# Tail scores ahead of the logits' weights in an attention and mixture-of-experts kernel, and the reads of their bank behind both

## The chip, the cores and the metric

The kernel runs on one core of one Trainium2 chip. The metric is the device time of one execution in microseconds (us), less is better. Every timed execution also records the span of its trace and the mean granted clock of TensorE. The quoted time is the median of a kernel's executions, "faster" and "slower" begin at 2%.

## The reference, cut to what matters

Causal attention over 8 batches x 8 heads, 576 positions of 64 elements, with a bias per pair of positions; then a mixture of 8 experts, in which each token goes to one expert.

```python
scores = scale * np.matmul(q, k.transpose(0, 1, 3, 2))
scores = np.where(causal, -1000000000.0, scores + np.minimum(bias, 0.0))
attn = np.exp(scores - max); attn = attn / (sum(attn) + 1e-09)
x = np.matmul(attn, v)                       # then (B, S, H*D)
logits = x @ w_gate; local_gate = sigmoid(x @ w_local)
# e = argmax(logits), or the expert of the token before where local_gate >= 0.5
out[b, s] = p[e] * (np.maximum(x[b, s] @ w1[e], 0.0) @ w2[e])
```

(shortened; `p` is the softmax of the logits.)

## The kernel before: the parts that matter

Attention goes over 32 pairs of heads, n = 0 to 31. 576 positions are four blocks of 128 and a tail of 64. The scores of the tail against itself are made apart, into columns of bank 1 of PSUM. The same bank takes the product of v with the weights of the logits ("gate"), and the tail's half of the product of the weights with v. The tokens' expert logits therefore come out of attention as extra columns of v.

In what follows, for pair n, S is its scores (L328), R the products of its weights with v (L402), G its products of v with the logits' weights (L366) and T its tail's scores (L351). A pass is the time from S of pair n to S of pair n + 1. PSUM, in banks, is where the program has TensorE put its products. In lines of the profile PE is TensorE, DVE VectorE, ACT ScalarE, POOL GpSimd and SP SyncE; "<-" in brackets names what ended a wait, and "issue" says that the profile shows nothing that was waited for. Each of these products stands in a trace as two records (the 20 of G as x40).

```python
def tail(n):
    ps = banks[1][:, TAIL : TAIL + TL]
    for h in range(2):
        d = slice(DH * h, DH * h + DH)
        mm(ps[d], lhsT=ins[n][1][:, TS:][:, d], rhs=ins[n][0][:, TS:], start=True, stop=True)   # L351
    sc = scs[n, "tail"] = p_sc.tile([P, TL], F32, name="tail")
    i = tail_bias + n
    nc.scalar.activation(sc, ps, Act.Exp, bias=bias[:, i : i + 1], scale=scale)                 # L354

def seen_tail(n):                                                                               # L358, on DVE
    ...
def gate_part(n):
    ps = banks[1][:, GATE : ...]
    ...                                     # 20 small products, bank 1 (L366)
    v = ins[n][3]
    nc.vector.tensor_copy(v[:, :, 1 : E + 2], ps[:, :, 0])                                      # L369
    nc.vector.tensor_copy(v[:, :, VW - E - 2 : VW - 1], ps[:, :, 1])                            # L370

def rows(n, g):                             # bank g
    ...                                     # products with v (L402), reciprocal (L404), multiply (L407)
    if g == 0 and hp == HP - 1:
        logits(b)                           # four DVE instructions, once in four pairs

tail(0)
for n in range(NPAIR + 1):
    load(n + 3)
    if n:
        seen_tail(n - 1)
    if n < NPAIR:
        for u, pieces in enumerate(...):    # three units
            scores(n, u)                    # L328
            weights(n, *pieces)             # 14 activations (L337) in all
    for f in plan.pop((n, 0), ()):
        f(bank)
    if n:
        rows(n - 1, 1)
        rows(n - 1, 0)
    ...
    if n < NPAIR:
        gate_part(n)
    if n + 1 < NPAIR:
        tail(n + 1)
    for half in (1, 2):
        for f in plan.pop((n, half), ()):
            f(bank)
```

(cut.) The `plan` holds the sort of the tokens: for four groups of batches, (0, 1), (2, 3), (4) and (5), their tokens' rows are scattered by expert while attention goes on, with indirect transfers that GpSimd issues, three in a pair of heads from n + 3 2/3 on (`i += 11`, L1018). The batches that are left follow after attention. Then come the experts.

## Time and profile before

| quantity | value |
|---|---|
| timed executions | 917.92, 919.64, 915.09 us |
| the execution that the profile shows | 860.34 us, span 858.6 us |
| TensorE busy | 813.0 us, 95% |
| TensorE waiting for L370, in T | 31.2 us, 31 times |
| attention ends | 295.35 us |
| sort's end and experts, after it | 563.2 us |

The profiled execution is not one of the timed ones and was 55 to 59 us faster than those.

### The profile page before, as it was taken

How to read it: one execution, taken by the hardware profiler on the slowest of the kernel's cores; microseconds unless marked ns; L12 is line 12 of the kernel's file. 1: busy time of each engine (PE TensorE's matmuls, PEld its weight loads, DVE VectorE, ACT ScalarE, POOL GpSimd, SP SyncE). 2: the span in 40 equal slices, each digit the busy share in tenths (PEclk: the TensorE clock that was granted, in tenths of full speed). 3: DMA queues.
4: the chain of work that ended last, by engine and by line, in shares of the span. 5: the costliest groups of instructions: out<-in, count | busy, mean ns of one | idle time of the engine just before them, and what ended most of it. 6: DMA issues, size and time to landing. Idle time of an engine off the chain costs nothing.

```text
span 858.6 us, 21153 instructions
## 1 busy us (share of the span) xinstructions
PE 813.0 (95%) x8793; PEld 603.9 (70%) x8793; DVE 210.3 (24%) x700; ACT 192.1 (22%) x535; POOL 174.1 (20%) x329
## 2 busy tenths in 40 slices
PE   9988989889888999999999999999999999999996
PEld 8777778777777885685667756676657756776762
DVE  2222432344343465301111111111111111111111
ACT  5655646557555300000000000000000000000000
POOL 3422235225434223101100011100011001100001
PEclk9999999999999999999999999999999999999999
DMA  9475448857555439996599566993689936996001
GB/s 317 141 234 159 156 138 269 319 197 226 188 165 215 168 107 333 402 396 216 179 359 391 217 235 227 360 386 146 236 302 379 371 132 231 322 409 235 20 14 40
DMA packets 64153, 204.64 MB, mean 238 GB/s; under 512 B 8269, under 2 KB 8301, under 8 KB 64048
## 3 DMA queue, kind: packets, MB, share of 16 engines
q1 hardware_dynamic: 55008, 172.41, 57.3%
q0 software_dynamic: 8896, 30.47, 9.4%
q8 instruction: 71, 1.16, 0.6%
q10 hardware_dynamic: 144, 0.33, 0.1%
q14 instruction: 34, 0.28, 0.1%
HBM read 179.93 MB, written 23.76 MB: 237 GB/s over the span
## 4 chain that ended last, share of the span: by engine, by line
PE 92%; DVE 3%; issue 2%; DMA 1%; ACT 1%; SPq 0%; POOL 0%; another core or an unknown queue 0%; POOLq 0%; ACTq 0%
PE yp L1200 31%; PE hp L1176 28%; PE o L402 12%; PE ps L328 11%; PE hp L1183 4%; PE xp L1059 2%; PE o L351 1%; PE o L366 1%; PE o L284 1%; DMA v<-in_vx_dram 1%; DVE v L369 1%; PE bank L930 1%; DMA x_rows<-r_empty 1%; PE bank L952 1%; DVE x L407 0%
## 5 line engine op out<-in xcount | busy, mean ns | idle before, releaser
L1200 PE MATMUL yp<-w,hT 128*128 128x512 f32 (+1 forms) x528 | 221.1, 594 | 0.0
L1176 PE MATMUL hp<-xT,w 128*128 128x256 f32 (+1 forms) x1088 | 192.1, 337 | 0.0
L1176 PEld LDWEIGHTS hp<-xT,w 128*128 128x128 f32 x1088 | 172.2, 191 | 23.7 <-issue 7.8
L337 ACT ACTIVATE sc<-ps,bias 128x256 f32<-128x256 f32 (+3 forms) x448 | 153.0, 471 | 36.4 <-PE ps L328 35.5
L1200 PEld LDWEIGHTS yp<-w,hT 128*128 128x128 f32 (+1 forms) x528 | 88.1, 181 | 100.4 <-issue 99.4
L1191 ACT ACTIVATE hT<-hp 128x512 f32<-128x512 f32 x38 | 22.7, 597 | 503.2 <-PE hp L1176 419.3
L1207 POOL DMA_INDIRECT out_dram<-y,at_gate x38 | 38.4, 1011 | 457.9 <-DVE y L1206 443.1
L402 PE MATMUL o<-v,sc 128*64 128x74 f32 x3072 | 113.9, 229 | 0.1
L402 PEld LDWEIGHTS o<-v,sc 128*64 128x64 f32 x3072 | 108.9, 136 | 7.3 <-issue 7.1
L328 PE MATMUL ps<-q,k 64*128 64x320 f32 (+2 forms) x768 | 102.5, 418 | 0.0
L343 POOL TENSOR_SCALAR_AFFINE_SELECT sc<-sc 128x256 f32<-128x256 f32 x160 | 65.8, 416 | 140.1 <-ACT sc L337 90.3
L328 PEld LDWEIGHTS ps<-q,k 64*128 64x128 f32 x768 | 77.2, 208 | 18.2 <-issue 2.7
L1189 DVE TENSOR_SCALAR hT<-hp 128x512 f32<-128x512 f32 x38 | 26.2, 689 | 220.4 <-PE hp L1176 187.7
L1200 PE MATMUL yp<-x,hT 128*128 128x512 f32 (+1 forms) x144 | 64.8, 595 | 0.0
L1206 DVE TENSOR_SCALAR y<-yp,at_gate 128x512 f32<-128x512 f32 x38 | 28.5, 751 | 135.5 <-PE yp L1200 135.5
L404 DVE RECIPROCAL recs<-o 128x4 f32<-128x4 f32 x64 | 12.1, 189 | 157.2 <-PE o L402 157.2
L1176 PEld LDWEIGHTS hp<-xT,x 128*128 128x128 f32 x320 | 46.1, 191 | 5.8 <-issue 2.6
L1176 PE MATMUL hp<-xT,x 128*128 128x128 f32 (+1 forms) x320 | 50.1, 317 | 0.0
L1018 POOL DMA_INDIRECT x_rows<-x,r_slot_i x40 | 38.7, 967 | 35.7 <-PE ps L328 19.7
L1067 DVE COPY xT<-xp 128x512 f32<-128x512 f32 x36 | 24.9, 691 | 81.1 <-PE xp L1059 81.0
L351 PE MATMUL o<-q,k 128*64 128x64 f32 x128 | 10.9, 250 | 31.2 <-DVE v L370 31.2
L1200 PEld LDWEIGHTS yp<-x,hT 128*128 128x128 f32 (+1 forms) x144 | 24.7, 178 | 21.3 <-issue 21.0
(160 smaller groups left out, 428.8 us busy)
## 6 DMA issues: line engine op xcount, KB each, us to landing
w<-in_w_dram SPq DMA_DIRECT2D x184, 512.0 KB, 9.7
x<-in_w_dram SPq DMA_DIRECT2D x56, 512.0 KB, 9.8
v<-in_vx_dram SPq DMA_DIRECT2D x32, 370.0 KB, 4.8
vt<-in_vz_dram SPq DMA_DIRECT2D x32, 320.0 KB, 3.5
k<-in_kz_dram SPq DMA_DIRECT2D x31, 320.0 KB, 5.1
q<-in_q_dram SPq DMA_DIRECT2D x32, 288.0 KB, 6.6
xg<-x_rows POOLq DMA_DIRECT2D x30, 293.0 KB, 8.5
x_rows<-r_empty SPq DMA_DIRECT2D x6, 293.0 KB, 5.4
```

The costliest lines, as they stand in the source:

```text
L328: mm(ps[:, h, at : at + z - a], lhsT=kb[d, c * P : c * P + P], rhs=qb[d, a:z], start=True, stop=True)
L337: nc.scalar.activation(scs[n, u][:, h, at : at + z - a], raw[u][:, h, at : at + z - a], Act.Exp, bias=bias[:, i : i + 1], scale=scale)
L343: nc.gpsimd.affine_select(out=x, in_=x, compare_op=Alu.is_ge, fill=0.0, base=0, pattern=[[0, 2], [1, P]], channel_multiplier=-1)
L402: mm(y, lhsT=w, rhs=x, start=start, stop=stop)
L1018: self.s.nc.gpsimd.indirect_dma_start(out=next(self.s.views)[:, :], out_offset=bass.IndirectOffsetOnAxis(ap=self.slot[:z, m : m + 1], axis=0),
L1067: nc.vector.tensor_copy(self.xT[i][:, :, k * P : k * P + P], self.ps)
L1176: mm(y, lhsT=w[0][:, c, f : f + P], rhs=xT[i][:, c, :], start=(c == 0), stop=(c == DK - 1))
L1183: mm(y[d, m], lhsT=w[h ^ swap][:, c, f + h * HALF : f + h * HALF + HALF], rhs=xT[i][:, c, m], start=(c == 0), stop=(c == DK - 1))
L1189: nc.vector.tensor_scalar_max(to, ps, 0.0)
L1200: mm(ps[n * m : n * m + m, :], lhsT=hT[i][:, c, a : a + m], rhs=wn[:, c, :], start=(c == 0), stop=(c == FK - 1))
L1206: nc.vector.tensor_scalar_mul(y, ps, gate[i, k])
L1207: nc.gpsimd.indirect_dma_start(out=next(outs)[:, :], out_offset=bass.IndirectOffsetOnAxis(ap=at[i, k][:, 0:1], axis=0), in_=y[:, :], eleme ...
```

## The change

The intent: T no longer waits for DVE to copy G's result out of their common bank, since T now comes before G; both copies come after both products. The logits no longer stand ahead of the copies on DVE. ACT's read of the tail goes behind the activations of the first unit of the next pass. The five scatters of the last group (batch 5) come one pair later.

```diff
-                i += 11
+                i += 11 if bs[-1] < 5 else 14
...
-    tail(0)
+    tail_scores(0)
     for n in range(NPAIR + 1):
         load(n + 3)
-        if n:
-            seen_tail(n - 1)
         if n < NPAIR:
             for u, pieces in enumerate((((0, 0), (3, 1)), ((0, 1), (1, 1)), ((2, 0), (2, 1), (1, 0)))):
                 scores(n, u)
                 weights(n, *pieces)
+                if u == 0:
+                    tail(n)
+            seen_tail(n)
...
+        if n + 1 < NPAIR:
+            tail_scores(n + 1)
         if n < NPAIR:
-            gate_part(n)
-        if n + 1 < NPAIR:
-            tail(n + 1)
+            gate_parts(n)
+            beside_v(n)
+        if n and n % HP == 0:
+            logits(n // HP - 1)
```

(cut: `tail` was split into `tail_scores`, the products, and `tail`, the activation; `gate_part` into `gate_parts`, the products, and `beside_v`, the copies; the call of `logits` left `rows`.)

More of the change, by code (lines that the diff above doesn't have):

```diff
@@ L344, in weights, with tail_scores, tail @@
                                             pattern=[[0, 2], [1, P]], channel_multiplier=-1)
-    def tail(n):
-        ps = banks[1][:, TAIL : TAIL + TL]
+    def tail_scores(n):
         for h in range(2):
             d = slice(DH * h, DH * h + DH)
-            mm(ps[d], lhsT=ins[n][1][:, TS:][:, d], rhs=ins[n][0][:, TS:], start=True, stop=True)
+            mm(banks[1][d, TAIL : TAIL + TL], lhsT=ins[n][1][:, TS:][:, d], rhs=ins[n][0][:, TS:], start=True, stop=True)
+    def tail(n):
         sc = scs[n, "tail"] = p_sc.tile([P, TL], F32, name="tail")
         i = tail_bias + n
-        nc.scalar.activation(sc, ps, Act.Exp, bias=bias[:, i : i + 1], scale=scale)
+        nc.scalar.activation(sc, banks[1][:, TAIL : TAIL + TL], Act.Exp, bias=bias[:, i : i + 1], scale=scale)
     def seen_tail(n):
@@ L358, in seen_tail, with gate_parts @@
         nc.vector.scalar_tensor_tensor(x, x, 3e38, seen, Alu.min, Alu.mult)
-    def gate_part(n):
-        ps = banks[1][:, GATE : GATE + NB * 2 * (E + 1)].rearrange("p (c h e) -> p c h e", c=NB, h=2)
+    gates = banks[1][:, GATE : GATE + NB * 2 * (E + 1)].rearrange("p (c h e) -> p c h e", c=NB, h=2)
+    def gate_parts(n):
         m = P // 4
@@ L365, in gate_part, with beside_v @@
             for j in range(0, P, m):
-                mm(ps[j : j + m, c], lhsT=ins[n][2][:, c * P + j : c * P + j + m], rhs=wz[:, n % HP],
+                mm(gates[j : j + m, c], lhsT=ins[n][2][:, c * P + j : c * P + j + m], rhs=wz[:, n % HP],
                    start=True, stop=True)
+    def beside_v(n):
         v = ins[n][3]
-        nc.vector.tensor_copy(v[:, :, 1 : E + 2], ps[:, :, 0])
-        nc.vector.tensor_copy(v[:, :, VW - E - 2 : VW - 1], ps[:, :, 1])
+        nc.vector.tensor_copy(v[:, :, 1 : E + 2], gates[:, :, 0])
+        nc.vector.tensor_copy(v[:, :, VW - E - 2 : VW - 1], gates[:, :, 1])
     def rows(n, g):
@@ L407, in rows @@
         nc.vector.tensor_tensor(x, y, rec.unsqueeze(3).to_broadcast([P, t1 - t0, 2, HW]), op=Alu.mult)
-        if g == 0 and hp == HP - 1:
-            logits(b)
     def logits(b):
```

## The prediction

> **What bounds the kernel now.** I read the page first (parts 1, 4 and the tail rows of part 5), then what TensorE waits for, then the timeline of one ordinary pair of heads, then the chain in order of time, then the clock by stretches. Names used below: for pair n, S(n) is its scores (L328), R(n) its products with v (L402), G(n) its products of v with the logits' weights (L366), T(n) its tail scores (L351). TensorE runs, per pass, S(n), R(n-1), G(n), T(n+1).
>
> ```profile
> span 858.6 us, 21153 instructions
> PE 813.0 (95%) x8793; PEld 603.9 (70%) x8793; DVE 210.3 (24%) x700; ACT 192.1 (22%) x535; POOL 174.1 (20%) x329
> ...
> PE 92%; DVE 3%; issue 2%; DMA 1%; ACT 1%; SPq 0%; POOL 0%; another core or an unknown queue 0%; POOLq 0%; ACTq 0%
> ...
> L351 PE MATMUL o<-q,k 128*64 128x64 f32 x128 | 10.9, 250 | 31.2 <-DVE v L370 31.2
> ```
>
> TensorE is the bound, 95% busy, 92% of the chain, so only time at which it stands still or runs slowly can be won. The last row is nearly all its recorded idle time: T waits 31.2 us in all for the second DVE copy (L370) that takes G's result out of PSUM. The list of TensorE's own waits says how often, and that nothing else comes near:
>
> ```profile
> PE o L351 <- DVE v L370: 31.2, 31, 2.2
> PE hp L1183 <- issue: 4.3, 3, 1.8
> PE o L284 <- POOL ident masks.py:199: 1.5, 1, 1.5
> ```
>
> One ordinary pass, lines from the timeline (start, us, engine, line; in brackets the idle time before):
>
> ```profile
> 21.50 0.54 PE L366 MATMUL o<-wz,vt 128*32 128x18 f32 x40
> 21.61 0.20 DVE L404 RECIPROCAL recs<-o 128x6 f32<-128x6 f32 x1 [0.48 <-PE o L402]
> 21.84 0.61 DVE L407 TENSOR_TENSOR x<-o,recs 128x438 f32<-128x438 f32 x1
> ...
> 22.48 0.19 DVE L370 COPY v<-o 128x45 f32<-128x45 f32 x1
> ...
> 22.73 0.34 PE L351 MATMUL o<-q,k 128*64 128x64 f32 x4 [0.69 <-DVE v L370]
> 23.00 2.86 PE L328 MATMUL ps<-q,k 64*128 64x320 f32 x24
> 23.11 0.31 ACT L354 ACTIVATE tail<-o,bias 128x64 f32<-128x64 f32 x1 [1.91 <-PE o L351]
> 24.24 4.78 ACT L337 ACTIVATE sc<-ps,bias 128x320 f32<-128x320 f32 x14 [0.81 <-PE ps L328]
> ```
>
> G is done at 22.04, but DVE must finish the reciprocal and the multiply of R first, so its copies end at 22.67 and T starts 0.06 us later: 0.69 us of TensorE idle. In passes with scatters it is about 0.95 us, and once in four passes, where the four DVE instructions of the logits stand ahead of the copies, about 2 us.
>
> There is a second, less visible loss. In the chain most S blocks take 2.79 us, but seven take 4.18, 4.38, 4.41, 4.44, 4.45, 4.32 and 4.21, at 48, 82, 109, 153, 181, 218 and 266 us. The view by stretches (us, busy time of PE, PEld, DVE, ACT, POOL, then the granted clock) explains it:
>
> ```profile
> 44.02:47.43 3.41, 1.31 (x65) 1.13 (x59) 2.55 (x10) 0.53 (x2) 0.79 (x2) 1.00 1.02 166
> 47.43:50.84 3.41, 3.27 (x18) 2.60 (x20) 0.21 (x2) 0.99 (x3) 0.00 (x0) 0.50 1.01 392
> 105.46:108.87 3.41, 2.72 (x81) 2.41 (x77) 1.35 (x5) 1.03 (x4) 1.03 (x4) 1.00 0.46 150
> 108.87:112.28 3.41, 3.41 (x20) 2.75 (x21) 1.30 (x7) 1.12 (x3) 0.43 (x3) 0.50 0.34 125
> 115.70:119.11 3.41, 1.70 (x76) 1.51 (x71) 2.62 (x10) 0.34 (x2) 0.60 (x2) 1.00 0.43 128
> 119.11:122.52 3.41, 3.19 (x28) 2.70 (x30) 2.11 (x11) 1.40 (x4) 0.00 (x0) 1.00 0.53 178
> ```
>
> Stretches of 3.41 us follow each other on a fixed grid; after a poor one the next runs at half clock. Five of the seven poor ones hold the long wait of a logits pass or one like it (1.3 to 1.7 us busy); the other kind (105.46) holds a 0.69 us wait plus G and a run of tiny sort products (L952, 1.3 us)[...]. A stretch with 1.70 us busy (115.70) escaped[...].
>
> [...] T writes other columns than L369 and L370 read, and yet waits, 31 times. So every read of this bank, ACT's of the tail included, orders TensorE's later writes. [...] here gaps of about 2 us within a window were enough (longest wait 2.2)[...].
>
> **The change, part by part.**
> 1. T(n+1) moves ahead of G(n), the copies behind both. T then needs of DVE only that R(n-1)'s part in this bank (done first in R) has been multiplied out. That is old: G stood there before and had the same need, and shows no DVE wait in the list. Removed: the 31 waits, -31.2 us.
> 2. The long gaps go, and the hold passes lose their 0.69 us, so I expect the poor stretches to go[...]. Seven S blocks sum to 30.39 us against 7 x 2.79 = 19.53: -10.9 us.
> 3. T streams behind R, which has the same 128x64 array tiling, and not after a standstill. From T's start to S's took 0.27 (22.73 to 23.00); in R an instruction costs 3.49 / 96 = 0.036, so four cost 0.15. About 0.1 x 31 = -3 us (estimate).
> 4. ACT's read of the tail moves from before the 14 activations to after the first four. Here lies the new wait: R(n-1) begins with the tail's bank, so it must wait for that read. In the pass above S starts at 23.00, R at 25.79. ACT begins at 24.24; the four take until 25.68 or so (the fifth one's start), the tail's activation 0.31, until 25.99, and the signal 0.06: R can start at 26.05, 0.26 us late. Nothing stands beside it on TensorE. 31 x 0.26 = +8.1 us.
> 5. In passes where the sort puts ACT work ahead (L941: ACT begins 1.60 us after S and not 1.24; L908 waits on DVE, which is now relatively later), the same wait grows by some 0.3 to 0.4, in about eight passes: +3 us (estimate).
> 6. The copies and the logits come later on DVE, but v is needed by R(n) only one S (2.79 us) later, and DVE is 34% busy in this stage: 0. The tail's masking (L358) gets earlier: the one 0.8 us wait of R on it goes; counted as nothing.
> 7. The last early group's five scatters move a pair later. Now the first one holds POOL 6.5 us for the early fetch of rows, and the masks of a pair queue behind it; that costs TensorE nothing today, with the passes 8 to 9 us long, but would be close with 7.3. A safeguard: 0.
>
> Sum: -31.2 - 10.9 - 3 + 8.1 + 3 = -34 us, all in the first 295 us. The expert stage (563 us, clock 1.00) has the same instructions and begins that much earlier. The timed 917.9 is 59 us above the profiled span; I take this as fixed. 917.9 - 34 = 883.9; I add 1 for one half-clock window that survives: 885 us.
>
> **The rivals.** (a) The wait moves wholly to ACT: if the tail's read is later than I place it, by 0.5 us or more, R stands 0.7 us or more in each pass and the change gives back over 20 us: about 898. Against it: ACT needs 14 activations plus a tail, 4.78 + 0.31 = 5.1 us, in a pass of about 7.3, so it does not fall behind. (b) The half-clock windows stay[...]: about 896. For it: the hold passes triggered with only 0.69 us of true idle. Against: the logits passes lose 2 us of true idle. (c) POOL or the loads become the bound. POOL in a scatter pass: five masks of 0.41 and three scatters of about 1.3 with their gaps, about 6 us, under 7.3. The loads of a pair are 1.3 MB, 178 GB/s at 7.3 us, where the trace moves 400 elsewhere, and they are issued three pairs ahead. If wrong: about 900. (d) No new wait at all, if the guard were by columns: about 875; the 31 waits of today speak against it.
>
> **Range and chances.** Items 1 and 2 are measured, and each can fail only in part; the sizes of 4 and 5 are the loose ones, perhaps 6 us either way, and the windows up to 8 the wrong way. Range 879 to 894. The 2% line lies at 899.6, 19 us of gain: it takes (a) or (c) to miss it. Faster 0.94, within 2% 0.055, slower 0.005.
>
> **What would show it.** The row of T without idle; a new row of waits of L402 on ACT's tail activation, about 31 times and 0.3 us; S blocks all near 2.8 us and the clock 1.00 from 15 us to the end of attention; ordinary passes 7.3 us apart instead of 7.76; the experts' 563 us unchanged; no scatter waiting for the early fetch. Wrong if R waits 0.6 us or more, if T waits for R's multiply (L407), if several stretches at 0.50 remain, or if the span fell by over 40 us.

## The result, and the profile after

| | before | changed |
|---|---|---|
| timed, median | 916.5 us (4 runs, 914.04 to 919.64) | 863.56 us (4 runs, 858.44 to 870.36) |
| ratio | | 0.9425, 95% interval 0.9346 to 0.9504 |

A ratio is the mean time of one kernel's runs over that of the other's of the same rounds, so not quite the ratio of the medians. The kernel became faster by 53 us. The predicted time was 885 us, with a range of 879 to 894; the result lies 15 us below the range.

Three lines of the changed kernel's page answer to those shown of before (busy times; the chain's shares; the group R, which has the line L406 now):

```profile
PE 811.8 (95%) x8793; PEld 600.0 (70%) x8793; DVE 214.5 (25%) x700; ACT 188.3 (22%) x535; POOL 173.4 (20%) x329
...
PE 89%; ACT 6%; issue 3%; DVE 1%; POOL 0%; POOLq 0%; ACTq 0%; DVEq 0%
...
L406 PE MATMUL o<-v,sc 128*64 128x74 f32 x3072 | 115.5, 231 | 17.1 <-ACT tail L355 15.7
```

T no longer stands idle, ACT stands in the chain with 6%, and R waits for ACT's tail activation: the old wait is gone and the expected new one is there, with 15.7 us instead of the 11 predicted. But the span of this profile is 856.8 us and that of the profile before was 858.6: the two profiles differ by 1.8 us, the two medians by 53. Two readings were open. Either the change gains little in the span and much outside it, or the two profiles are of different conditions. The second predicts that, on one and the same chip, spans and times of both kernels differ by the same amount.

### The profile page after: what moved, and what is told of

Its sections match the earlier page's. It is cut to its first block, busy times and chain, and to the rows that moved or that the text cites.

```text
span 856.8 us, 21067 instructions
## 1 busy us (share of the span) xinstructions
PE 811.8 (95%) x8793; PEld 600.0 (70%) x8793; DVE 214.5 (25%) x700; ACT 188.3 (22%) x535; POOL 173.4 (20%) x329
## 4 chain that ended last, share of the span: by engine, by line
PE 89%; ACT 6%; issue 3%; DVE 1%; POOL 0%; POOLq 0%; ACTq 0%; DVEq 0%
PE yp L1207 31%; PE hp L1183 28%; PE o L406 13%; PE ps L328 7%; ACT sc L337 5%; PE hp L1190 4%; PE xp L1066 2%; PE o L368 2%; PE o L284 1%; PE bank L959 1%; PE bank L937 1%; ACT tail L355 1%; PE o L349 1%; DVE r_u L947 0%; ACT r_v L948 0%
## 5 line engine op out<-in xcount | busy, mean ns | idle before, releaser
L337 ACT ACTIVATE sc<-ps,bias 128x256 f32<-128x256 f32 (+3 forms) x448 | 156.9, 482 | 80.4 <-PE ps L328 78.3
L406 PE MATMUL o<-v,sc 128*64 128x74 f32 x3072 | 115.5, 231 | 17.1 <-ACT tail L355 15.7
L406 PEld LDWEIGHTS o<-v,sc 128*64 128x64 f32 x3072 | 110.7, 138 | 26.4 <-ACT tail L355 24.4
L328 PEld LDWEIGHTS ps<-q,k 64*128 64x128 f32 x768 | 72.8, 189 | 26.5 <-issue 11.3
L1190 PEld LDWEIGHTS hp<-xT,w 128*64 128x64 f32 x768 | 30.9, 138 | 6.2 <-issue 6.2
L411 DVE TENSOR_TENSOR x<-o,recs 128x292 f32<-128x292 f32 x64 | 34.5, 538 | 2.2
```

The source lines that it names most:

```text
L328: mm(ps[:, h, at : at + z - a], lhsT=kb[d, c * P : c * P + P], rhs=qb[d, a:z], start=True, stop=True)
L337: nc.scalar.activation(scs[n, u][:, h, at : at + z - a], raw[u][:, h, at : at + z - a], Act.Exp, bias=bias[:, i : i + 1], scale=scale)
L406: mm(y, lhsT=w, rhs=x, start=start, stop=stop)
L411: nc.vector.tensor_tensor(x, y, rec.unsqueeze(3).to_broadcast([P, t1 - t0, 2, HW]), op=Alu.mult)
L1190: mm(y[d, m], lhsT=w[h ^ swap][:, c, f + h * HALF : f + h * HALF + HALF], rhs=xT[i][:, c, m], start=(c == 0), stop=(c == DK - 1))
```

## The experiments

Thirteen runs. Kernels of one call ran on one chip and share the runs of the kernel before.

| run | chip | before, us | this, us | ratio | 95% interval |
|---|---|---|---|---|---|
| e1 before again | 4 | 863.17 | 862.24 | 1.0004 | 0.9948 to 1.006 |
| e2 changed again | 4 | 863.17 | 827.38 | 0.9584 | 0.9539 to 0.9629 |
| e3 scatters alone | 4 | 863.17 | 864.34 | 1.001 | 0.9956 to 1.0063 |
| e4 order alone | 4 | 863.17 | 829.51 | 0.9624 | 0.9581 to 0.9667 |
| e5 early read | 1 | 862.48 | 823.18 | 0.9547 | 0.9509 to 0.9585 |
| e6 changed, third | 1 | 862.48 | 828.73 | 0.9593 | 0.9544 to 0.9641 |
| e7 filled waits | 1 | 862.48 | 852.09 | 0.9878 | 0.9838 to 0.9918 |
| e8 logits later | 1 | 862.48 | 847.62 | 0.9825 | 0.9784 to 0.9866 |
| e9 before, other chip | 15 | 912.55 | 911.15 | 0.9985 | 0.9822 to 1.0147 |
| e10 changed, other chip | 15 | 912.55 | 856.76 | 0.9389 | 0.9217 to 0.956 |
| e11 before, scatters moved | 3 | 912.1 | 912.67 | 1.0012 | 0.9966 to 1.0058 |
| e12 changed, scatters moved | 3 | 912.1 | 863.59 | 0.9474 | 0.9418 to 0.953 |
| e13 early read again | 3 | 912.1 | 836.37 | 0.9175 | 0.908 to 0.9271 |

Theory A: the predicted mechanism is complete (about 34 us), and the first measurement met a condition in which the kernel before loses more. Rival B: part of the change that was taken for nothing (the scatters, the place of the logits) is worth 20 us. Rival C: the timed executions carry a cost outside the span that the change removes. (In the expectations of e1 and e2, "theory A" is another one: the fixed cost outside the span, as the prediction had it.)

### Both kernels again, and the two parts of the change (e1 to e4)

e1 and e2 are the two kernels without an edit. e3 is the kernel before with the scatters' line alone, e4 the changed kernel without it:

```diff
# e3, from before                              # e4, from changed
-                i += 11                       -  i += 11 if bs[-1] < 5 else 14
+                i += 11 if bs[-1] < 5 else 14 +  i += 11
```

> The unchanged kernel once more. Question: is its profiled span of 858.6 us (execution 860.3) typical, with 916 us in the timed executions? Theory A (a fixed cost outside the trace, as I had predicted): the profiled execution again near 860 and the timed ones near 916 with spans near 859. Theory B (the kernel before has a slower mode that its first profile missed): timed spans near 915 with a lower granted clock or more standing still inside the span, and with luck this profile falls into it. Ratio to the kernel before 1.00 either way.

> The changed kernel once more. Theory A: profiled and timed executions between 858 and 870 again, clock 0.98 to 0.99. Stalls of 1 to 5 us that the first profile shows at TensorE without a releaser (for instance at 132 and 190 us) are either at the same instructions again (then they belong to the program[...]) or elsewhere (then they belong to the execution).

> The kernel before with the last early group's five scatters one pair later and nothing else. My theory: this part alone is a safeguard and gives nothing (within 0.5% of before, 910 to 920 timed). Rival: the scatter that holds POOL 6.5 us, waiting for the early fetch of rows, is what puts the kernel before into its slow timed mode; then this one is near 865.

> The changed kernel with the scatters left where they were. My theory: all of the gain is in the order of the tail scores, so within 0.7% of the changed kernel (858 to 872). Rival: as above, then near 900 or more.

On this chip the kernel before took 863.17 us, not 917, and the changed kernel 827.38: 35.8 us less. The timed figures that the expectations of e1 to e4 had for these kernels (about 916, 858 to 870, 910 to 920, 858 to 872) were all missed, since they were those of the first measurement. (e3's 864 is near what its rival named, but the kernel before took as long on this chip.) The profiled and the timed executions of e1 agree (863.13 and a median of 862.24), which neither of its theories had. Spans moved with it, from 861.4 to 826.4 (-35.0). Rival C falls: what the timed runs show, the span shows. The prediction's own sum, taken from its own profile, 858.6 - 34 = 825, meets the span of 826.4. Rival B falls for the scatters: alone they moved nothing (ratio 1.001), and with the new order they gave 2.1 us at most (829.51 against 827.38), with intervals that overlap; whether that is real stays open. Both runs are of an ordinary chip. What the later scatters are worth in the slower condition was not run.

One ordinary pass of the changed kernel, from e2's timeline (start, us, engine, line; idle time before in brackets), answers the pass in the prediction:

```profile
58.52 0.54 PE L368 MATMUL o<-wz,vt 128*32 128x18 f32 x40
...
58.99 2.86 PE L328 MATMUL ps<-q,k 64*128 64x320 f32 x24
...
60.23 1.57 ACT L337 ACTIVATE sc<-ps,bias 128x320 f32<-128x320 f32 x4 [2.32 <-PE ps L328]
...
61.68 0.33 ACT L355 ACTIVATE tail<-o,bias 128x64 f32<-128x64 f32 x1
...
62.06 0.99 PE L406 MATMUL o<-v,sc 128*64 128x74 f32 x24 [0.21 <-ACT tail L355]
```

S follows G at once: 58.99, within the recorded span of G, where before T stood still for 0.69 us. ACT starts S's first four activations 1.24 us after S, reads the tail at 61.68 to 62.01, and R starts 0.05 us later. S would have let R start at 61.78 (2.79 us after 58.99, as before), so R is late by 0.28 us; the bracket calls 0.21 of it idle, since the recorded end of S is a little later. From S to S this pass lasts 66.13 - 58.99 = 7.14 us, before 7.76.

The rows that carry the sum, first of e1, then of e2 (busy us, mean ns; idle us before, and what ended it):

```profile
L328 PE MATMUL ps<-q,k 64*128 64x320 f32 (+2 forms) x768 | 102.8, 419 | 0.0
...
L351 PE MATMUL o<-q,k 128*64 128x64 f32 x128 | 10.8, 248 | 30.0 <-DVE v L370 30.0
```

```profile
L406 PE MATMUL o<-v,sc 128*64 128x74 f32 x3072 | 113.6, 229 | 7.5 <-ACT tail L355 6.9
...
L328 PE MATMUL ps<-q,k 64*128 64x320 f32 (+2 forms) x768 | 95.2, 392 | 2.8 <-issue 2.4
```

Read together: T's 30.0 us gone, R's 6.9 us new, S shorter by 7.6 us because the blocks at half clock went (seven stretches at half clock in attention before, one after; the mean granted clock of that stage went from 0.96 to 0.99). The question that e2 put, whether TensorE's waits without a releaser ("issue") come again at the same instructions, has an answer: those of 0.3 us and more in attention stand in passes 15, 18, 29 and 31 both in e2 and in e6 on another chip (e2 has one more in pass 23, e6 one in pass 20), the one in pass 18 in the middle of G (1.01 and 1.55 us). Most of them thus belong to the program; what they wait for is not shown.

### Two losses and the new wait, one at a time (e5 to e8)

e7 leaves T's waits in place and fills the long ones with products of the identity that nobody reads, so that only the clock can gain:

```diff
# e7, from before
         if n < NPAIR:
             gate_part(n)
+        if n in (4, 8, 11, 16, 19, 20, 12, 23, 24, 27, 28):
+            idle = bank(1)[0]
+            for i in range(6 if n % HP == 0 else 2):
+                mm(idle[:, :P], lhsT=ident, rhs=ident, start=True, stop=True)
```

e8 takes from the change only the place of the logits on DVE; e5 lets ACT read the tail right behind DVE's copies, before the next S has activations; e6 is the changed kernel unedited, beside them.

```diff
# e8, from before: the call of logits leaves rows, and
         if n < NPAIR:
             gate_part(n)
+        if n and n % HP == 0:
+            logits(n // HP - 1)
# e5, from changed
     tail_scores(0)
+    tail(0)
...
-                if u == 0:
-                    tail(n)
...
             beside_v(n)
+        if n + 1 < NPAIR:
+            tail(n + 1)
```

> The changed kernel, but ACT's read of the tail stands right behind DVE's copies, ahead of the pair's 14 activations, where ACT is idle. My theory: the new wait of R on the tail's activation (0.27 us in each of 31 passes) goes, nothing takes its place, so about 7 to 8 us less than the changed kernel, ratio to before near 0.950 where the changed kernel is at 0.958. Rival: the read now waits for the copies of DVE in the same bank and pushes the 14 activations back, so that nothing is gained or the scores' buffers come free too late (ratio 0.96 or more).

> The changed kernel a third time, beside the others, and on whichever chip this call gets. If the chip is like the one of the second run: 827 us and ratio 0.958. If it is like the one of the first (before at 916): 864 and 0.943, and then its profile shows more standing still of TensorE without a releaser, most of it in the first 290 us.

> The kernel before with its waits left as they are, but the long ones (logits passes) and those of the sort's hold passes filled with 6 and 2 products that nobody reads, so that TensorE is busy while it waits. My theory: the half-clock windows go, the waits stay (31 of them, about 30 us less what the fill covers), and the kernel gains 8 to 11 us, ratio 0.987 to 0.991. Rival: half clock costs nothing of its own because the slow scores are hidden behind ACT; then ratio 1.00.

> The kernel before with nothing changed but the place of the logits' four DVE instructions: behind the copies and not ahead of them. My theory: the seven long waits fall from about 2.0 to 0.7 us (about 9 us) and the four or five half-clock windows behind them go (about 7 us): 14 to 17 us, ratio 0.980 to 0.984; 31 waits remain, of about 0.7 to 0.95 us. Rival: the windows stay, since G and the wait still make a poor stretch: ratio 0.989 or more.

e7 gained 10.4 us (862.48 to 852.09) by adding work; by the 2% rule it counts as the same and e8 as unclear, but the intervals of both exclude a ratio of 1. Its row of S says why:

```profile
L328 PE MATMUL ps<-q,k 64*128 64x320 f32 (+2 forms) x768 | 93.7, 389 | 0.3 <-issue 0.3
```

S fell from 102.8 to 93.7 us, and one stretch of attention instead of seven ran at half clock (mean granted clock of the stage 0.99, in e1 0.96). That is close to the predicted -10.9, alone and on purpose.

e8 gained 14.9 us: T's waits fell from 30.0 to 24.4 us, S from 102.8 to 94.8.

```profile
L351 PE MATMUL o<-q,k 128*64 128x64 f32 x128 | 10.7, 246 | 24.4 <-DVE v L370 24.4
```

The place of the logits, of which the prediction spoke only as the long wait once in four passes, is therefore a large part: it shortens six of the seven long waits to 0.7 us (that of pass 4 stays at 2.2) and leaves two stretches at half clock in attention instead of seven (mean granted clock 0.99). The rest of the change brings 18.9 us more (847.62 to e6's 828.73 on the same chip). How the gain divides depends on which part comes first; with T ahead of G, T waits for no copy wherever the logits stand, and the logits' place was not run there. The gains of e8 and e7 overlap and can't be added.

e5 removes the new wait wholly. Its pass from the timeline:

```profile
58.36 0.20 DVE L374 COPY v<-o 128x45 f32<-128x45 f32 x1
...
58.65 0.31 ACT L355 ACTIVATE tail<-o,bias 128x64 f32<-128x64 f32 x1 [2.70 <-DVE v L374]
...
60.76 0.99 PE L406 MATMUL o<-v,sc 128*64 128x74 f32 x24
```

ACT is free at that moment (idle 2.70 us), reads the tail at 58.65, and R starts at 60.76, 2.79 us after S at 57.97, with no bracket. An ordinary pass lasts 6.85 us instead of 7.13 (the measure of the new wait: 0.28 a pass), and the kernel 823.18 us against 828.73 of the changed kernel on the same chip. That is 5.5 us, where 7 to 8 were expected, and the intervals against before overlap: of the times the gain is not clear, of the wait it is (no line of e5 shows R waiting for ACT's read).

### The other condition (e9 and e10)

By now two chips had given 34 to 36 us where the first measurement gave 53. The kernel before had taken 862 and 863 us, not 917. e9 and e10 are the two kernels unedited, sent to whatever chip came next.

> The kernel before once more, to meet the condition of the first measurement (916 us), whose trace is missing. If this call gets an ordinary chip: 860 to 867 and nothing new. If it gets one like the first: about 916, and the trace then tells between (a) longer waits at the places that the change removes, T on L370 well above 31 us, or (b) standing still without a releaser, spread over both stages, as in the first trace of the changed kernel.

> The changed kernel beside it on the same chip: about 828 on an ordinary chip, about 864 on one like the first, ratio 0.958 or 0.943.

This chip, 15, showed the first measurement's times: 911.15 and 856.76 us, and this time with profiles of both (spans 904.7 and 849.8, a gain of 54.9). The rows of e9, then of e10:

```profile
L328 PE MATMUL ps<-q,k 64*128 64x320 f32 (+2 forms) x768 | 118.0, 467 | 0.0
...
L351 PE MATMUL o<-q,k 128*64 128x64 f32 x128 | 11.6, 264 | 47.9 <-DVE v L370 47.9
```

```profile
L406 PE MATMUL o<-v,sc 128*64 128x74 f32 x3072 | 113.7, 229 | 19.0 <-ACT tail L355 17.6
...
L328 PE MATMUL ps<-q,k 64*128 64x320 f32 (+2 forms) x768 | 101.1, 395 | 5.4 <-issue 2.7
```

Against e1, T's waits have grown from 30.0 to 47.9 us, the longest from 2.2 to 4.2, and S from 102.8 to 118.0, with fourteen stretches at half clock in attention instead of seven, six of them two windows of 3.41 us long (mean granted clock of the stage 0.89, in e1 0.96). Nearly all of the 43.3 us between the spans of e9 and e1 lies before the end of R: 336.77 - 295.69 = 41.1. And it is not spread out. Durations from S to S, in us:

| pass | 2 | 13 | 14 | 15 | 17 | 19 | 22 | 23 |
|---|---|---|---|---|---|---|---|---|
| e1, before on chip 4 | 7.77 | 8.05 | 8.03 | 8.04 | 9.42 | 9.02 | 9.11 | 9.12 |
| e9, before on chip 15 | 7.77 | 12.51 | 12.82 | 13.15 | 9.45 | 9.02 | 15.27 | 14.22 |
| e2, changed on chip 4 | 7.14 | 7.13 | 7.13 | 7.92 | 7.16 | 8.67 | 8.37 | 10.32 |
| e10, changed on chip 15 | 7.13 | 7.19 | 10.01 | 10.05 | 7.13 | 8.67 | 12.62 | 11.41 |

(S of pair n to S of pair n + 1 is pass n.) Passes 2, 17 and 19 are equal on both chips. Long are those in which scatters are issued: passes 12 to 15, 20 to 23, 24 to 26 and 28 to 30 (29 to 31 in the changed kernel), and the one behind. In sum, passes 12 to 16 are 17.2 us longer in e9 than in e1, passes 20 to 30 together 26.0, all others 1.8 shorter. Pass 13 of e9's timeline shows what happens there; the same pass of e1 stands below it:

```profile
126.32 0.54 PE L366 MATMUL o<-wz,vt 128*32 128x18 f32 x40
...
126.66 0.61 DVE L407 TENSOR_TENSOR x<-o,recs 128x438 f32<-128x438 f32 x1
...
129.04 0.97 POOL L1018 DMA_INDIRECT x_rows<-x,r_slot_i  x1 [0.30 <-issue]
...
130.71 0.20 DVE L369 COPY v<-o 128x45 f32<-128x45 f32 x1 [3.44 <-remote]
...
131.08 0.34 PE L351 MATMUL o<-q,k 128*64 128x64 f32 x4 [4.22 <-DVE v L370]
```

```profile
127.08 0.61 DVE L407 TENSOR_TENSOR x<-o,recs 128x438 f32<-128x438 f32 x1
...
127.89 0.20 DVE L369 COPY v<-o 128x45 f32<-128x45 f32 x1 [0.19 <-PE o L366]
...
128.26 0.34 PE L351 MATMUL o<-q,k 128*64 128x64 f32 x4 [0.97 <-DVE v L370]
```

("remote": the profile found no instruction close by that gave the signal.) In e1 the first copy starts 0.20 us after DVE's multiply. In e9 DVE has nothing else to do from 127.27 on, and G's record ends at 126.86; yet the copy starts at 130.71, 0.70 us after the record of the third scatter of the pass ends (129.04 + 0.97 = 130.01). T follows 0.37 us later, as in e1. SyncE, which waits for G too before it loads into that buffer, goes on at 130.70, and the trace has TensorE's own semaphore raised at 130.69: so it is the word from TensorE that G is done which comes late. Whether the word alone was late, or TensorE's completing of G, the trace can't tell, since the ends of its products are modelled.

The changed kernel on that chip is held up in the same way, as a pass of e10 shows:

```profile
121.25 3.52 PE L328 MATMUL ps<-q,k 64*128 64x320 f32 x21
...
123.47 0.98 POOL L1025 DMA_INDIRECT x_rows<-x,r_slot_i  x1 [0.31 <-issue]
...
125.16 0.60 PE L328 MATMUL ps<-q,k 64*128 64x192 f32 x3 [0.38 <-issue]
...
125.26 0.20 DVE L373 COPY v<-o 128x45 f32<-128x45 f32 x1 [3.65 <-PE ps L328]
...
125.42 1.57 ACT L337 ACTIVATE sc<-ps,bias 128x320 f32<-128x320 f32 x4 [5.06 <-PE ps L328]
...
127.24 0.99 PE L406 MATMUL o<-v,sc 128*64 128x74 f32 x24 [1.49 <-ACT tail L355]
```

Here the third scatter's record ends at 124.45, the copy starts 0.81 us later and ACT 0.97: both of TensorE's readers are late together; ACT begins 4.17 us after S, where it takes 1.24 in an ordinary pass. But TensorE has S to do meanwhile: it starts at 121.25, right behind G. S is slowed as well, at a granted clock of 1.00: it lasts until 125.76, 4.50 us instead of 2.86. Then R stands, 1.49 us. Together, less the 0.21 us of an ordinary wait, these are the 2.92 us by which this pass (15) is longer than an ordinary one (10.05 against 7.13). Why S is slowed is not shown; more than a signal may be held back. In the kernel before, the same delay leaves TensorE 4.22 us with nothing, and half clock behind it (S then takes 4.55 us; the mean granted clock from 133 to 146 us is 0.76).

The delay is not one of DVE alone: in the pass of e10 ACT (125.42) and SyncE's next load (125.26) go on as late as DVE's copy (125.26). A remark on reading: the third scatter's record ends before its data have moved. On the queue of these transfers (`prof e9_before_chip --dma --window 127:132`) packets move in three blocks, the third from 130.59 to 131.50, so from 0.58 us after the third record's end (in e1 the records of the scatters last 0.90 to 1.03 us, and their data land 2.7 to 7.6 us after issue). TensorE's signal comes 0.1 us into that block and does not wait for its end. Nor does it always wait for the third scatter: in three other passes of e9 it came as the third record ended.

### Does the loss follow the scatters (e11 to e13)?

If the scatters make the loss and not, say, the sort's DVE work of these passes, then moving the first group's scatters two pairs later must move the loss, in both kernels:

```diff
# e11, from before                             # e12, from changed
-  i += 11                                     -  i += 11 if bs[-1] < 5 else 14
+  i += 17 if bs == (0, 1) else 11             +  i += 17 if bs == (0, 1) else 11 if bs[-1] < 5 else 14
```

e13 is e5's kernel again, in the other condition.

> The kernel before with the ten scatters of the first group two passes later (14.2 to 17.2 in place of 12.2 to 15.2), nothing else. On the slow chip (before near 912) passes 12 to 15 took 11.7, 12.5, 12.8 and 13.2 us where an ordinary chip takes 11.3, 8.0, 8.0 and 8.0. Theory S (the scatters hold back TensorE's signals on such a chip): passes 12 and 13 fall to about 9 and 8 us, and passes 14 to 17 hold the excess. Theory L (something at that time, such as the traffic of loads, or that stretch of instructions): passes 12 and 13 stay above 11. On an ordinary chip (before near 863) nothing but the small cost of three scatters in a pass moves, and the total stays within 1%.

> The changed kernel with the same move. On a slow chip passes 14, 15 and 16 took 10.0 to 10.1 us and 12 and 13 were ordinary (7.7 and 7.2), because the copies whose signal is late are waited for only after the next scores. Theory S: the passes of 10 us move two passes on (16 and 17 at least, 14 then at 7.1). Theory L: they stay at 14 to 16. On an ordinary chip all of them are 7.1 to 8.

> The version with ACT's read of the tail behind the copies, which was fastest on an ordinary chip (823, changed kernel 829). On a slow chip: theory S says that its read, which waits for DVE's copies, which wait for TensorE's late signal, comes late too, but no later than the scores' own activations, whose signal is as late; so it stays 4 to 8 us ahead of the changed kernel, about 852 with before at 912. Ordinary chip: 816 to 824 again.

| pass | 13 | 14 | 15 | 16 | 17 | 18 | 19 |
|---|---|---|---|---|---|---|---|
| e9, before | 12.51 | 12.82 | 13.15 | 11.45 | 9.45 | 9.23 | 9.02 |
| e11, before, moved | 10.37 | 8.84 | 11.09 | 15.23 | 13.21 | 11.11 | 9.03 |
| e10, changed | 7.19 | 10.01 | 10.05 | 10.09 | 7.13 | 10.04 | 8.67 |
| e12, changed, moved | 7.13 | 7.13 | 7.42 | 14.58 | 7.13 | 13.78 | 8.67 |

The loss moved: in the kernel before, passes 13 and 14 shed most of it and 16 to 18 took it on; in the changed kernel, passes 14 and 15 shed it and 16 and 18 took it on. The total of the kernel before stayed (ratio 1.0012). Two limits of this comparison: e9 and e10 are of chip 15 and e11 to e13 of chip 3 (before: 912.55 and 912.1 us), and pass 13 of e11 stayed at 10.37, where 8 was expected, with a stretch at half clock (from 120.2 us on) at its start, as in e3's on an ordinary chip (10.39). The figure for pass 12 in the expectation, about 9, was a slip: that pass takes 11.3 us in e1 and 11.9 in e3 without any such loss, and took 11.9 in e11.

e13 gives 836.37 us, a ratio of 0.9175, where the change itself had 0.9389 on chip 15 and, with moved scatters, 0.9474 on chip 3. The expectation, about 852, was too high: R waits for ACT's read 1.4 us in all in e13, and 17.6 in e10 (chip 15), so the early read takes out most of what the late signals add to that wait. The early read is thus the best version of both conditions (823 and 836 us), by 5.5 us of the changed kernel on chip 1; in the slower condition it wasn't run beside the unedited changed kernel.

## Why the prediction was wrong

**The step that failed.** It is the last one: "The timed 917.9 is 59 us above the profiled span; I take this as fixed." It carried the sum from the profiled execution, 858.6 us, over to the timed ones. The 59 us were not fixed; where a profile met the slower condition (e9), 41.1 of the 43.3 us that it has over e1 lie in attention, and T's waits and S, slowed by half clock, the very things that the change removes, grew by 17.9 and 15.2 us. In the condition of the profile the change gave 35.8 us (e2), in that of the timed runs 53 to 55 (first result, e10 against e9). 916.5 - 53 is the result.

What showed it beforehand: the record of the profiled execution has its own time, 860.34 us, 1.8 above its span. A fixed cost outside the span would have been in there too. The right reading was that two conditions existed and that the timed ones had some 57 us more of something; the range should then have been wide on the low side, since what a slower condition adds may well be what the change takes away.

**The sum itself, in the profile's condition.** Predicted -34, measured -35.8 in time and -35.0 in span. By its steps:

1. T's waits, -31.2: right. e1 has 30.0, e2 none.
2. The half clock, -10.9: right as a size. S fell by 7.6 us between e1 and e2, with one stretch that stayed; e7, which does nothing else, gained 10.4. The reading behind it was loose. Of the seven poor stretches four and not five hold a long wait (1.31, 1.48, 1.48 and 1.69 us busy), three are of the other kind (2.60 to 2.72). And busy time alone sets no limit: in the same profile the stretch at 262.47 with 1.69 us was followed by half clock, that at 187.38 with 1.65 was not.
3. T streaming behind R, -0.1 a pass: too small. The ordinary pass went from 7.76 to 7.13. Of this -0.63, the wait gave -0.69 and R's new delay +0.28, so about -0.2 is left for it: some -6 us and not -3 (an estimate from those three numbers). The timelines show it as the time from R's start to that of the block behind it: 3.48 us in e1 (G), 3.27 in e2 (T).
4. R behind ACT's read, +0.26 a pass: right. e5 measures 0.28, of which the profile of e2 records 0.21 as idle in an ordinary pass.
5. Longer waits in sort passes, +3: right. In eight passes of e2 R waits 0.40 to 0.49 us, together 2.1 more than eight ordinary waits. In eight others no wait is recorded, so items 4 and 5 sum to 6.9 us in 23 passes and not to 11.1. In addition some waits called "issue" came, which the sum did not have: 5.4 us before G and S in e2 against 1.6 in e1.
6. and 7. Nothing from the copies, the logits' cost or the scatters: right for the scatters by e3, on an ordinary chip. The logits' place is worth 14.9 us by itself (e8), but through items 1 and 2. (The 2% line, 899.6, lies 18.3 us under 917.9 and not 19.)

With the rows of the two profiles: -30.0 (T) - 7.6 (S) - 6 (streaming) + 6.9 (R) + 3.8 (issue) = -32.9 us, and attention from 15.30 us to R's end went from 280.39 to 247.49 us, by -32.9. That the two agree to the tenth is luck, as the term of streaming is an estimate. The other 2.1 us of the spans' difference lie behind attention, where nothing was changed (565.7 in e1, 563.7 in e2, 563.2 in the first profile of before).

**The sum in the slower condition.** The same rows of e9 and e10: -47.9 (T) - 16.9 (S) - 6 + 17.6 (R) - 0.8 (issue before G and S: 5.1 in e9, 4.3 in e10) = -54.0 us, measured -53.5 in attention (321.47 to 268.02). Some 4 us of smaller waits in e10 are left out, so it is no closer than that. The two terms that differ from the ordinary chip by most are T's waits and S at half clock. TensorE's signals are held back in the scatters' passes for both kernels (DVE idle for 3.44 us ahead of the copy in pass 13 of e9, for 3.65 in pass 15 of e10); the kernel before has nothing to run then, the changed one has S, slowed as it is (4.50 us for 2.86). Chip 15 cost the kernel before 41.1 us of attention over chip 4 and the changed kernel 20.5.

**The rivals.** (a), (b) and (c), all of them for a smaller gain, did not occur on the ordinary chip: R waited 0.3 us and not 0.7, one stretch at half clock was left, no load and no GpSimd work came to bound a pass of 7.13 us. In the slower condition (a) did happen in part (17.6 us of waits of R, longest 3.1), beside a gain that was larger still. (d), no new wait, did not occur. What the prediction's list lacked was a rival for a larger gain, and its last line, "if the span fell by over 40 us", names just what came, in a condition that its profile did not show.

**What stays open.** Which chip made the first measurement is not recorded; that its timed runs were of the condition of e9 to e13 is inferred from their times (917 and 864 us against 911 and 857), from the profile of the changed kernel (passes 14 to 16 of 9.9 to 10.2 us, R's waits 15.7 us) and from nothing else. Why the scatters hold back TensorE's signals on two chips and hardly on two others was not found: the scatters could not be taken out without leaving rows unwritten or racing, so they were moved only. Nor is it shown that the rest of the time between two conditions, after waits and half clock, has the same cause.

## What to carry to other kernels

Before a sum from a profile is put on a timed figure, compare the time of the profiled execution itself with the timed ones: a difference between them (59 us here) was a second condition of which the profile showed nothing, and the gain there has to be a range of its own. When an engine that sets the end waits once in each pass for another engine's copy, put work between the two that depends on neither; it hid the wait of the ordinary condition (30.0 us in e1) and about half of what the slower one added (41.1 us of attention before, 20.5 after). Long waits cost twice where half clock follows them (granted 0.50 for 3.41 us), so shortening six rare ones (the logits, once in four pairs) brought 14.9 us, when all the rest of the change brought 18.9.

## What the traces show of the chip

- Stretches at half clock (3.41 us at a granted clock of 0.50) followed waits of 2.2 us and less; filling eleven waits with two or six products that nobody reads gained 10.4 us (e7), shortening six long ones 14.9 (e8). Neither the longest wait nor the busy time of a stretch of 3.41 us decides alone: stretches with 1.31 and with 2.72 us busy were followed by half clock, one with 1.70 was not (all three in the prediction), and in e1 a wait of 0.7 us in pass 11 was followed by it, those of 1.9 us in passes 12 and 24 were not.
- On two chips of four, passes in which GpSimd issued indirect scatters one behind the other were longer (pass 22: 15.27 us in e9 on chip 15, 9.11 in e1 on chip 4; pass 17 on chip 3 with the scatters moved into it: 13.21 in e11, 9.45 in e9). In two of them, shown above, TensorE's completion signals reached DVE, ACT and SyncE late, 0.7 to 1.0 us after the last scatter's record ended. A copy started after 3.44 us of idle instead of 0.19 (e9, e1), and activations 4.17 us after S instead of 1.24 (e10, e2).
- The same kernel on one core took 863 us on two chips and 912 us on two others, with 41.1 of 43.3 us of the difference in one stage. The mean granted clock was 0.981 in e1 and 0.959 in e9; in the changed kernel it was 0.996 on both (e2, e10), with spans of 826.4 and 849.8 us.
- T writes other columns of bank 1 than L369 and L370 read, and waited for L370 31 times (31.2 us in the first profile of before); R waits for ACT's read of the tail in the same bank (6.9 us in 23 passes of e2). No run here left that order out.
